# Hash attention followed by a max-out FFN: the projection split on POOL, and pair 1's hash in one pass

## The chip, the cores and the metric

The kernel runs on one core of a Trainium2 chip. A core has five engines that work side by side, each through its own queue in order: TensorE (PE, matrix multiplication), VectorE (DVE), ScalarE (ACT), GpSimd (POOL) and SyncE (SP, here only the issuer of DMAs). They wait for each other on semaphores. The metric is device time in microseconds (us), the median of several runs; lower is better.

## The reference

Attention for 4 batches of 8 heads, 768 positions and 64 dimensions, in which a query sees only the keys of its own hash bucket, and then a feed-forward network on all 3072 tokens:

```python
q_bits = (np.einsum('bhsd,dk->bhsk', q, proj) > 0)       # 6 bits, the same for k
mask = q_bucket[:, :, :, None] == k_bucket[:, :, None, :]
scores = np.where(mask, scale * q @ k.T, -1e9)
attn = exp(scores - max) / (sum + 1e-09)
x = (attn @ v) -> [3072, 512]
h = np.maximum(np.maximum(x @ w1, x @ w2), x @ w3)       # 512 -> 768
out = h @ w_out                                          # 768 -> 512
```

The sign of a projection decides a bit, so the projections are formed to nearly fp32 accuracy: q, k and the projection are each taken apart into an fp16 number and an fp16 remainder.

## The kernel before

**Tiling.** Heads are taken in pairs (b, pr): batch b, pair pr of 0 to 3. For each pair q, k and v are loaded by SP (`load`, L250, 384 KB each). `split_h` (L266 on ACT, L268 on DVE) writes the fp16 part, `split_r` (L273, DVE) the remainder beside it, 24 chunks of 128 positions (2 for q and k, 2 heads, 6 chunks). The chunks are transposed to the tile `T`, with dimension and remainder on 128 partitions: on PE (`pe_T` L292, evacuated by `evac_T` on DVE or ACT, L204 or L202) for batch 0 and the first two pairs of batch 1, by a DMA transpose on SP (`xbar`, L282) for the rest.

**The hash.** `hash_mm` multiplies each chunk of `T` with `PAB`, the 12 columns of the split projection (6 of the fp16 part, 6 of the remainder), which `make_p` (L234 to L239) builds once on DVE. It has two forms. "Summed" (L310) runs two matmuls of 6 columns into the same 6 outputs, 48 per pair; `hash_bits0` then compares them with zero in one DVE instruction. The other (L312) runs one matmul of 12 columns, 24 per pair; `hash_bits` negates the second six (L330) and compares the first six with them (L332). Pairs 0 and 1 of batch 0 are summed, all others take one pass. The bits, scaled, become six more rows of the score product, so that the scores of other buckets vanish in the exponential. For pair (0,0) they go into `S16` and are transposed a second time; for all others they are transposed on PE (L339), written by SP to DRAM (`bit_out`, dr<-bt, L349) and read back into `T` (`bit_in`, T<-dr, L352). This is called the bounce here.

**Attention.** A unit is one score product (L395, two matmuls), one exponential on ACT (`expo`, L401, 128x768) and one product with v (`attend`, L413, six matmuls). There are 192 units, 48 per batch. PSUM holds two score tiles, so the score of unit n waits for the exponential of unit n - 2. `norm_t` and `norm_x` divide by the sums on DVE. The value sums (`vsum` on POOL L363 to L366, `mean_mm` on PE, svp) belong to the masked positions.

**FFN.** `l1` (L478) and `l2` (L496) work on half batches; `l1_evac` takes the maximum on DVE. The weights come in half by half: w1, w2 and w3 as (half, matrix). Most are loaded by a DMA on the POOL queue that converts to fp16 (`load_w`, L541); those named in `plain`, and w_out in three parts, are loaded by SP into the staging tile ws (`stage_w`, L663, two buffers) and converted by POOL (`cast_w`, L204).

**The order.** Nothing is written in order by hand. Every step is a task for `Plan.run`, with a cost in us for its engine, a priority, its inputs and the buffers that it takes and gives. The planner plays the tasks through with these costs and emits on each engine the ready task of the lowest priority number. The result is a fixed program for each queue. A changed cost can therefore change the order of everything behind it. While PE has no ready task before the first score, `keep_warm` emits a filler matmul (wps, L771).

Of the kernel before, what the change touches and what calls it, by code (L numbers as in the profile page):

```python
# [10 lines left out]
AluOp = mybir.AluOpType  # L11
# [16 lines left out]
class Plan:  # L28
# [105 lines left out]
def kernel(  # L134
# [12 lines left out]
    nc = tc.nc  # L147
    B, H, S, D = q.shape
    NBITS = proj.shape[1]
# [9 lines left out]
    NA = 4 * NCH  # L159
# [27 lines left out]
    op = ctx.enter_context(tc.tile_pool(name="op", bufs=OSB))  # L187
# [9 lines left out]
    add = plan.add  # L197
# [8 lines left out]
    p32 = konst.tile([D, NBITS], FP32, name="p32")  # L206
# [16 lines left out]
    PAB = konst.tile([P, 2 * NBITS], FP16, name="PAB")  # L223
# [7 lines left out]
    def make_p(e):  # L231
        ph = konst.tile([D, NBITS], FP16, name="ph")
        pr32 = konst.tile([D, NBITS], FP32, name="pr32")
        nc.vector.tensor_copy(ph[:], p32[:])  # L234
        nc.vector.tensor_tensor(out=pr32[:], in0=p32[:], in1=ph[:], op=AluOp.subtract)
        for o in (0, D):
            for i, src in enumerate((ph, pr32)):
                nc.vector.tensor_scalar(out=PAB[o : o + D, NBITS * i : NBITS * (i + 1)], in0=src[:],
                                        scalar1=1024.0, scalar2=None, op0=AluOp.mult)  # L239


    raws, S16, T, bits, bts, drs, pss = {}, {}, {}, {}, {}, {}, {}
    src = {"q": q, "k": k, "v": v}

    def load(n, b, pr, heads, e):
        h0, h1 = heads
        if (n, b, pr) not in raws:
            raws[n, b, pr] = raw.tile([P, 2, NCH * D], FP32, tag=n + "32", name=n + "32")
        x = src[n][b, 2 * pr + h0 : 2 * pr + h1]
        ENG[e].dma_start(raws[n, b, pr][:, h0:h1, :], x.rearrange("h (p c) d -> p h (c d)", c=NCH))  # L250
# [8 lines left out]
    def split_h(n, b, pr, heads, e):  # L259
        if (b, pr) not in S16:  # L260
            S16[b, pr] = spl.tile([P, NA, 2 * D], FP16, tag="s", name="s")
        a0, a1 = chunks(n, heads)
        o = S16[b, pr][:, a0:a1, 0:D]
        x32 = raw_view(n, b, pr, heads)
        if e == "ACT":
            nc.scalar.activation(o, x32, ActFn.Copy, scale=QS)  # L266
        else:
            ENG[e].tensor_scalar(out=o, in0=x32, scalar1=QS, scalar2=None, op0=AluOp.mult)  # L268
# [12 lines left out]
    def xbar(b, pr, e):  # L281
        nc.sync.dma_start_transpose(operand(b, pr)[:], S16[b, pr][:].rearrange("p a d -> p (a d)"))  # L282

    def bank(key, name):
        pss[key] = mm_ps.tile([P, 512], FP32, tag="mm", name=name)
        return pss[key]
# [10 lines left out]
        copy(e, operand(b, pr)[:, a0:a1, :].rearrange("p a t -> p (a t)"), p16[:, 0 : NCH * P])  # L297

    def hash_mm(b, pr, heads, e):
        hps = bank(("h", b, pr), "hps")  # L300
        summed = 4 * b + pr < 2
        K = NBITS if summed else 2 * NBITS
        for n in range(2):
            for hh in range(*heads):
                for c in range(NCH):
                    a = n * NA2 + hh * NCH + c
                    o = hps[:, a * K : (a + 1) * K]
                    if summed:
                        for i in range(2):
                            nc.tensor.matmul(o, T[b, pr][:, a, :], PAB[:, i * K : (i + 1) * K], start=i == 0, stop=i == 1)  # L310
                    else:
                        nc.tensor.matmul(o, T[b, pr][:, a, :], PAB[:], start=True, stop=True)  # L312

    def hash_bits0(pr, heads, e):
        hv = pss.pop(("h", 0, pr))[:, 0 : NA * NBITS].rearrange("p (n a k) -> p n a k", n=2, k=NBITS)
        sl = slice(heads[0] * NCH, heads[1] * NCH)
        bit = small.tile([P, 2, NA2, NBITS], FP16, tag="bit", name="bit")
        if pr:
            bits[0, pr] = bit
            nc.vector.tensor_scalar(out=bit[:], in0=hv, scalar1=0.0, scalar2=None, op0=AluOp.is_gt)  # L320
            return
        nc.vector.tensor_scalar(out=bit[:, :, sl, :], in0=hv[:, :, sl, :], scalar1=0.0, scalar2=0.5,  # L322
                                op0=AluOp.is_gt, op1=AluOp.subtract)
        nc.vector.tensor_scalar(out=S16[0, pr][:].rearrange("p (n a) d -> p n a d", n=2)[:, :, sl, D : D + NBITS],
                                in0=bit[:, :, sl, :], scalar1=2 * BIT, scalar2=None, op0=AluOp.mult)

    def hash_bits(b, pr, e):
        hv = pss.pop(("h", b, pr))[:, 0 : NA * 2 * NBITS].rearrange("p (a k) -> p a k", k=2 * NBITS)
        neg = small.tile([P, NA, NBITS], FP32, tag="neg", name="neg")
        nc.vector.tensor_scalar(out=neg[:], in0=hv[:, :, NBITS : 2 * NBITS], scalar1=-1.0, scalar2=None, op0=AluOp.mult)  # L330
        bits[b, pr] = bit = small.tile([P, 2, NA2, NBITS], FP16, tag="bit", name="bit")
        nc.vector.tensor_tensor(out=bit[:].rearrange("p n a k -> p (n a) k"), in0=hv[:, :, 0:NBITS], in1=neg[:],  # L332
                                op=AluOp.is_gt)

    def bit_T(b, pr, e):
        bit = bits.pop((b, pr))
        p16 = bank(("b", b, pr), "bps")[:].bitcast(FP16)
        for n in range(2):
            nc.tensor.transpose(p16[0:R, n * P : (n + 1) * P], bit[:, n, :, :].rearrange("p a k -> p (a k)"), iden[:])  # L339
# [183 lines left out]
    def both(dve, act):  # L523
        return [("DVE", dve), ("ACT", act)]
# [7 lines left out]
    for i, (n, pr, heads) in enumerate(order):  # L532
        half = heads != (0, 2)
        loads[n, 0, pr, heads] = add(("SP", 0.45), -400 + i, [], lambda e, n=n, pr=pr, heads=heads: load(n, 0, pr, heads, e),
                                     take=(n,) if heads[0] == 0 else (), xfer=0.55 if half else 1.1)
    mp = add(("DVE", 0.5), -300, [add(("ACT", 0.1), -500, [], lambda e: None, lat=3.2)], make_p)

    def load_w(i, half, e):
        w_ap = (moe_w1, moe_w2, moe_w3)[i].rearrange("(c p) f -> p c f", p=P)
# [21 lines left out]
    def prep(b, pr):  # L561
        U = first_unit[b, pr]
        p0 = U - PRE
        by_pe = b == 0 or b == 1 and pr < 2
        if b > 0:
            for n in "qkv":
                g = divmod(4 * b + pr - GATE, 4)
                if b == 1:
                    g = {("q", 0): (0, 2), ("k", 0): (0, 2)}.get((n, pr), (0, 3) if pr < 3 else (1, 0))
                loads[n, b, pr, (0, 2)] = add(("SP", 0.5), U - 44 + 0.1 * "qkv".index(n), [],  # L570
                                              lambda e, n=n: load(n, b, pr, (0, 2), e), take=(n,), xfer=1.1, pad=2 if 4 * b + pr > 5 else 0.0,
# [31 lines left out]
        ev, both_rs = [], []  # L603
        last = None
        for i, n in enumerate("qk"):
            h = add(both(0.53, 0.72), p0 + 0.1 * i, [loads[n, b, pr, (0, 2)]],
                    lambda e, n=n: split_h(n, b, pr, (0, 2), e), take=("s",) if n == "q" else (),
                    after=[last])
            rs = [add(("DVE", 0.54), p0 + 1 + 0.1 * i, [h, last], lambda e, n=n, hh=hh: split_r(n, b, pr, (hh, hh + 1), e),
                      give=(n,) if hh else ()) for hh in range(2)]  # L610
            last = rs[1]
            if by_pe:
                for hh in range(2):
# [3 lines left out]
                                  give=("mm",)))  # L617
            both_rs += rs
        if not by_pe:
            ev = [add(("SP", 0.6), p0 + 2, both_rs, lambda e: xbar(b, pr, e), pad=4, xfer=4.6, hold=3.4, take=("T",))]  # L620
            xbars[4 * b + pr] = ev[0]
        plan.join(ev, ("s",))
        hm = add(("PE", 1.3 if 4 * b + pr < 2 else 0.67), p0 + 4, ev + [mp], lambda e: hash_mm(b, pr, (0, 2), e), take=("mm",))
        hb = add(("DVE", 0.3 if 4 * b + pr < 2 else 0.62), p0 + 5, [hm],
                 (lambda e: hash_bits(b, pr, e)) if 4 * b + pr >= 2 else (lambda e: hash_bits0(pr, (0, 2), e)), take=("bit",), give=("mm",))
        bT = add(("PE", 0.11), p0 + 6, [hb], lambda e: bit_T(b, pr, e), take=("mm",), give=("bit",))
        be = add(("DVE", 0.28), p0 + 6, [bT], lambda e: bit_evac(b, pr, e), take=("bt",), give=("mm",))
        bo = add(("SP", 0.65), p0 + 7, [be], lambda e: bit_out(b, pr, e), take=("dr",), give=("bt",), xfer=0.05,
# [17 lines left out]
        t = small.tile([P, 1], FP16, tag="hold", name="hold")  # L646
        nc.gpsimd.tensor_copy(t[D : D + NBITS, :], T[b, pr][D : D + NBITS, NA - 1, P - 1 : P])

    plain = ((1, 2),)
    wst_tiles = {}  # L650

    def w_view(w, i):
# [69 lines left out]
    for blk, (b, pr, items) in enumerate(blocks):  # L722
# [6 lines left out]
        for slot in range(2):  # L729
            for j in range(NU):  # L730
                hf, hh = items[slot]
                s = add(("PE", 0.33), u, ready_T[b, pr, hh], lambda e, u=u: score(u, e), take=("sc",), after=[prev_s],
                        give=("T",) if blk == last_block[b, pr] and slot == 1 and j == NU - 1 else ())
# [4 lines left out]
                              take=("av",) if slot == 0 and j == 0 else (), give=("at",))  # L738
                u += 1
        if blk == last_block[b, pr]:  # L740
# [6 lines left out]
                 take=() if b == 0 or (b, hf) in has_xn else ("xn",), after=has_xn.get((b, hf), []) if b else [])  # L747
# [58 lines left out]
```

The softmax here doesn't subtract the row's maximum and nothing guards it: scores larger than these inputs give would overflow.

## Time and profile before

| What | Value |
|---|---|
| Median of 4 runs | 268.09 us (267.53 to 268.93) |
| The profiled execution | 268.34 us, span of its instructions 266.5 us |
| PE, ACT, DVE, POOL busy | 258.1, 196.3, 177.6, 41.1 us |
| Mean granted TensorE clock | 0.993 |
| Bytes moved by DMA | 41.69 MB |
| First score matmul | 13.60 us after the start of the span |

The times of the trace count from the start of the span. A busy share is an average over very different stages: up to 13.6 us the first pair is prepared, until about 48 us there is attention alone, then attention and FFN run interleaved, and from about 212 us there is FFN alone. PE counts as busy while it runs fillers too.

### The profile page before, as it was taken

To read this page: it belongs to the slowest core of one execution; us is meant where nothing else is said; L and a number is where in the kernel's file an instruction comes from. 1 tells how busy PE (TensorE), PEld (TensorE's weight loads), DVE (VectorE), ACT (ScalarE), POOL (GpSimd) and SP (SyncE) were. 2 spreads that over 40 slices of the span, in tenths; PEclk is the share of its full clock that TensorE was granted. 3 is DMA by queue.
4 is the path that set the end of the run, shared out by engine and by line. 5 is a ranking of instruction groups with operands and counts; after the bars stand their busy time and mean duration, and the time that the engine had idled before them with its cause. 6 is when DMAs were issued, how large, how long until landed. Compare 5 with 4: busy or idle time off the path is not lost.

```text
span 266.5 us, 7323 instructions
## 1 busy us (share of the span) xinstructions
PE 258.1 (97%) x2992; PEld 176.5 (66%) x2992; DVE 177.6 (67%) x394; ACT 196.3 (74%) x283; POOL 41.1 (15%) x57
## 2 busy tenths in 40 slices
PE   8799999999989999999999999999999999999995
PEld 8788777767646666677666767765666656555552
DVE  4799789998856898559886796551655535345260
ACT  4689999987926989999989889898899642332422
POOL 1430053173310333003321030000000000000000
PEclk9799999999999999999999999999999999999999
DMA  6994489699998698997995796212130050120303
GB/s 194 369 269 73 137 270 265 183 258 296 222 241 268 199 241 195 208 254 204 181 245 143 232 182 121 54 29 79 42 61 0 4 163 15 42 79 0 121 0 119
DMA packets 67408, 41.69 MB, mean 156 GB/s; under 512 B 48046, under 2 KB 63662, under 8 KB 67374
## 3 DMA queue, kind: packets, MB, share of 16 engines
q1 hardware_dynamic: 64654, 39.26, 57.5%
q0 software_dynamic: 2640, 1.97, 4.8%
q8 instruction: 23, 0.38, 0.6%
q14 instruction: 11, 0.09, 0.1%
q10 hardware_dynamic: 80, 0.00, 0.0%
HBM read 25.72 MB, written 6.84 MB: 122 GB/s over the span
## 4 chain that ended last, share of the span: by engine, by line
PE 78%; DMA 11%; DVE 3%; ACT 2%; POOL 2%; SPq 2%; issue 1%; ACTq 0%; POOLq 0%
PE ps L478 31%; PE sc L395 19%; PE po L496 11%; PE av L413 10%; DMA v<-in_v_dram 3%; PE tps L292 3%; PE hps L312 2%; DMA dr<-bt 2%; DMA q<-in_q_dram 2%; DMA ws<-in_moe_w_dram 2%; DMA ws<-in_moe_w_out_dram 2%; ACT AT L401 2%; SPq L250 1%; DVE s L273 1%; DVE s L268 1%
## 5 line engine op out<-in xcount | busy, mean ns | idle before, releaser
L401 ACT ACTIVATE AT<-sc 128x768 f16<-128x768 f32 x192 | 146.2, 814 | 15.2 <-PE sc L395 13.3
L478 PE MATMUL ps<-xT,w_sb 128*128 128x384 f16 x576 | 106.3, 326 | 0.0
L395 PE MATMUL sc<-T 128*128 128x384 f16 x384 | 93.0, 326 | 0.9 <-ACT AT L401 0.4
L487 DVE TENSOR_TENSOR ht<-ht,ps 128x384 f16<-128x384 f16 x96 | 52.9, 551 | 46.3 <-PE ps L478 43.8
L413 PEld LDWEIGHTS <-AT 128*128 128x128 f16 x1152 | 59.5, 97 | 22.7 <-ACT AT L401 0.2
L478 PEld LDWEIGHTS <-w_sb 128*128 128x128 f16 x576 | 52.7, 98 | 30.8 <-issue 0.7
L413 PE MATMUL av<-vone,AT 128*128 128x65 f16 x1152 | 65.5, 193 | 0.0
L395 PEld LDWEIGHTS <-T 128*128 128x128 f16 x384 | 30.3, 97 | 11.7 <-issue 1.3
L496 PE MATMUL po<-wout_sb,ht 128*128 128x512 f16 (+1 forms) x150 | 33.8, 370 | 1.0 <-POOL wout_sb L204 1.0
L202 ACT CAST ht<-ps 128x384 f16<-128x384 f32 x28 | 13.4, 480 | 26.4 <-DVE ht L487 19.1
L202 ACT COPY osb<-po 128x512 f32<-128x512 f32 (+1 forms) x24 | 13.6, 568 | 19.3 <-PE po L496 19.2
L496 PEld LDWEIGHTS <-ht 128*128 128x128 f16 x150 | 14.1, 98 | 14.8 <-DVE rr L436 1.2
L273 DVE SCALAR_TENSOR_TENSOR s<-q,s 128x384 f16<-128x384 f32 x32 | 21.2, 676 | 4.1 <-ACT s L266 3.9
L363 POOL TENSOR_TENSOR vt<-v 128x384 f32<-128x384 f32 x12 | 13.3, 1111 | 67.2 <-DMA v<-in_v_dram 67.1
L430 DVE TENSOR_TENSOR t<-av,mv 128x390 f32<-128x390 f32 x32 | 17.9, 560 | 7.3 <-PE av L413 7.0
L449 DVE TENSOR_TENSOR xn<-t,rr 128x384 f16<-128x384 f32 x32 | 19.7, 617 | 1.1
L273 DVE SCALAR_TENSOR_TENSOR s<-k,s 128x384 f16<-128x384 f32 x32 | 18.5, 597 | 0.2
L204 DVE CAST ht<-ps 128x384 f16<-128x384 f32 x20 | 11.1, 555 | 10.4 <-PE ps L478 10.1
L292 PE MATMUL tps<-iden,s 128*128 128x128 f16 x168 | 14.7, 233 | 1.7 <-DVE bit L322 1.5
L292 PEld LDWEIGHTS <-s 128*128 128x128 f16 x168 | 11.6, 105 | 2.9 <-DVE s L273 1.7
L202 ACT CAST vone<-v 128x768 f16<-128x768 f32 x12 | 10.0, 834 | 0.9 <-DMA v<-in_v_dram 0.9
L312 PEld LDWEIGHTS <-T 128*128 128x128 f16 x336 | 10.0, 96 | 1.0
(54 smaller groups left out, 144.9 us busy)
## 6 DMA issues: line engine op xcount, KB each, us to landing
v<-in_v_dram SPq DMA_DIRECT2D x16, 384.0 KB
out_dram<-osb SPq DMA_DIRECT2D x23, 256.0 KB
q<-in_q_dram SPq DMA_DIRECT2D x15, 384.0 KB
k<-in_k_dram SPq DMA_DIRECT2D x15, 384.0 KB
w_sb<-in_moe_w_dram POOLq DMA_DIRECT2D x5, 384.0 KB, 10.0
ws<-in_moe_w_out_dram SPq DMA_DIRECT2D x3, 512.0 KB
ws<-in_moe_w_dram SPq DMA_DIRECT2D x2, 384.0 KB
dr<-bt SPq DMA_DIRECT2D x15, 36.0 KB
```

Source lines behind the costliest of these rows:

```text
L202: nc.scalar.copy(o, i)
L273: nc.vector.scalar_tensor_tensor(out=s[:, a0:a1, D : 2 * D], in0=raw_view(n, b, pr, heads), scalar=QS, in1=s[:, a0:a1, 0:D], op0=AluOp.mul ...
L292: nc.tensor.transpose(p16[:, c * P : (c + 1) * P], S16[b, pr][:, a0 + c, :], iden[:])
L312: nc.tensor.matmul(o, T[b, pr][:, a, :], PAB[:], start=True, stop=True)
L395: nc.tensor.matmul(sc[:, i, 0:HQ], t[:, NA2 + hh * NCH + 2 * j + i, :], t[:, hh * NCH + hf * CH : hh * NCH + (hf + 1) * CH, :], start=True ...
L401: nc.scalar.activation(AT[:], scs.pop(u)[:, :, 0:HQ], ActFn.Exp, bias=EXP_BIAS, scale=EXP_SCALE)
L413: nc.tensor.matmul(av[:, o : o + D + 1], AT[:, i, c * P : (c + 1) * P], vones[b % 2][:, 2 * pr + hh, 2 * j + i, 0 : D + 1], start=slot == ...
L430: nc.vector.tensor_tensor(out=t[:, :, :, 0 : D + 1], in0=av[:, :, :, 0 : D + 1], in1=mv, op=AluOp.add)
L449: nc.vector.tensor_tensor(out=xv, in0=t[:, :, :, 0:D], in1=rr[:].to_broadcast([P, 2, CH, D]), op=AluOp.mult)
L478: nc.tensor.matmul(ps[:, 0:HQ], w_sb[i][:, jc, fb * P : (fb + 1) * P], xTs[b, hf][:, jc, :], start=jc == 0, stop=jc == NJ - 1)
L487: nc.vector.tensor_tensor(out=ht[:], in0=ht[:], in1=ps[:, 0:HQ], op=AluOp.max)
L496: nc.tensor.matmul(ps[:, m0:m1], hts[b, hf, fb][:, c * P : (c + 1) * P], wout_sb[:, fb, m0:m1], start=fb == 0, stop=fb == NF - 1)
```

## The change

Four edits in one. `make_p` moves to POOL, and its task is booked there with 1.5 us instead of 0.5 us on DVE. Pair 1 of batch 0 takes the one-pass hash, so that only pair 0 is still summed; its compare is then `hash_bits` with two DVE instructions. The PSUM tiles of the hash are told apart by head, so that both heads of pair 0 can be under way at a time. And `plain` gains (1, 1): the second half of w2 is loaded by SP through the staging tile and converted on POOL, as the second half of w3 was already.

```diff
     def make_p(e):
-        nc.vector.tensor_copy(ph[:], p32[:])
-        nc.vector.tensor_tensor(out=pr32[:], in0=p32[:], in1=ph[:], op=AluOp.subtract)
+        nc.gpsimd.tensor_copy(ph[:], p32[:])
+        nc.gpsimd.tensor_tensor(out=pr32[:], in0=p32[:], in1=ph[:], op=AluOp.subtract)
         for o in (0, D):
             for i, src in enumerate((ph, pr32)):
-                nc.vector.tensor_scalar(out=PAB[...], in0=src[:],
+                nc.gpsimd.tensor_scalar(out=PAB[...], in0=src[:],
                                         scalar1=1024.0, scalar2=None, op0=AluOp.mult)
...
     def hash_mm(b, pr, heads, e):
-        hps = bank(("h", b, pr), "hps")
-        summed = 4 * b + pr < 2
+        hps = bank(("h", b, pr, heads[0]), "hps")
+        summed = 4 * b + pr < 1
...
-    mp = add(("DVE", 0.5), -300, [...], make_p)
+    mp = add(("POOL", 1.5), -300, [...], make_p)
...
-        hm = add(("PE", 1.3 if 4 * b + pr < 2 else 0.67), ...
-        hb = add(("DVE", 0.3 if 4 * b + pr < 2 else 0.62), p0 + 5, [hm],
-                 hash_bits if 4 * b + pr >= 2 else hash_bits0 ...
+        hm = add(("PE", 1.3 if 4 * b + pr < 1 else 0.67), ...
+        hb = add(("DVE", 0.3 if 4 * b + pr < 1 else 0.62), p0 + 5, [hm],
+                 hash_bits if 4 * b + pr >= 1 else hash_bits0 ...
...
-    plain = ((1, 2),)
+    plain = ((1, 1), (1, 2))
```

More of the change, by code (lines that the diff above doesn't have):

```diff
@@ L233, in make_p @@
         pr32 = konst.tile([D, NBITS], FP32, name="pr32")
-        nc.vector.tensor_copy(ph[:], p32[:])
-        nc.vector.tensor_tensor(out=pr32[:], in0=p32[:], in1=ph[:], op=AluOp.subtract)
+        nc.gpsimd.tensor_copy(ph[:], p32[:])
+        nc.gpsimd.tensor_tensor(out=pr32[:], in0=p32[:], in1=ph[:], op=AluOp.subtract)
         for o in (0, D):
             for i, src in enumerate((ph, pr32)):
-                nc.vector.tensor_scalar(out=PAB[o : o + D, NBITS * i : NBITS * (i + 1)], in0=src[:],
+                nc.gpsimd.tensor_scalar(out=PAB[o : o + D, NBITS * i : NBITS * (i + 1)], in0=src[:],
                                         scalar1=1024.0, scalar2=None, op0=AluOp.mult)
@@ L314, in hash_bits0 @@
     def hash_bits0(pr, heads, e):
-        hv = pss.pop(("h", 0, pr))[:, 0 : NA * NBITS].rearrange("p (n a k) -> p n a k", n=2, k=NBITS)
+        hv = pss.pop(("h", 0, pr, heads[0]))[:, 0 : NA * NBITS].rearrange("p (n a k) -> p n a k", n=2, k=NBITS)
         sl = slice(heads[0] * NCH, heads[1] * NCH)
@@ L327, in hash_bits @@
     def hash_bits(b, pr, e):
-        hv = pss.pop(("h", b, pr))[:, 0 : NA * 2 * NBITS].rearrange("p (a k) -> p a k", k=2 * NBITS)
+        hv = pss.pop(("h", b, pr, 0))[:, 0 : NA * 2 * NBITS].rearrange("p (a k) -> p a k", k=2 * NBITS)
         neg = small.tile([P, NA, NBITS], FP32, tag="neg", name="neg")
@@ L535 @@
                                      take=(n,) if heads[0] == 0 else (), xfer=0.55 if half else 1.1)
-    mp = add(("DVE", 0.5), -300, [add(("ACT", 0.1), -500, [], lambda e: None, lat=3.2)], make_p)
+    mp = add(("POOL", 1.5), -300, [add(("ACT", 0.1), -500, [], lambda e: None, lat=3.2)], make_p)
     def load_w(i, half, e):
@@ L622, in prep @@
         plan.join(ev, ("s",))
-        hm = add(("PE", 1.3 if 4 * b + pr < 2 else 0.67), p0 + 4, ev + [mp], lambda e: hash_mm(b, pr, (0, 2), e), take=("mm",))
-        hb = add(("DVE", 0.3 if 4 * b + pr < 2 else 0.62), p0 + 5, [hm],
-                 (lambda e: hash_bits(b, pr, e)) if 4 * b + pr >= 2 else (lambda e: hash_bits0(pr, (0, 2), e)), take=("bit",), give=("mm",))
+        hm = add(("PE", 1.3 if 4 * b + pr < 1 else 0.67), p0 + 4, ev + [mp], lambda e: hash_mm(b, pr, (0, 2), e), take=("mm",))
+        hb = add(("DVE", 0.3 if 4 * b + pr < 1 else 0.62), p0 + 5, [hm],
+                 (lambda e: hash_bits(b, pr, e)) if 4 * b + pr >= 1 else (lambda e: hash_bits0(pr, (0, 2), e)), take=("bit",), give=("mm",))
         bT = add(("PE", 0.11), p0 + 6, [hb], lambda e: bit_T(b, pr, e), take=("mm",), give=("bit",))
```

## The prediction

> **What bounds the kernel now.** I read the page's first two parts, then busy time by stage, then what the TensorE queue (PE) waited for, then the chain that ended last, then the SP queue in order of time. Busy time by stage (PE, weight loads, DVE, ACT, POOL, then granted clock, DMA share, GB/s):
>
> ```profile
> 6.90:10.30 3.40, 1.90 (x47) 1.82 (x45) 1.87 (x6) 2.00 (x4) 0.00 (x0) 1.00 1.04 364
> 10.30:13.70 3.40, 3.40 (x53) 3.40 (x51) 3.34 (x7) 1.97 (x3) 3.17 (x5) 0.50 1.07 377
> 13.70:28.00 14.30, 14.24 (x273) 12.26 (x272) 13.52 (x31) 13.16 (x19) 2.79 (x3) 1.00 0.75 152
> 28.00:48.00 20.00, 19.02 (x321) 14.61 (x317) 17.57 (x43) 19.68 (x28) 6.30 (x9) 1.00 0.85 226
> 48.00:77.00 29.00, 27.53 (x334) 18.55 (x331) 25.83 (x55) 23.14 (x34) 11.50 (x14) 1.00 1.03 247
> 77.00:264.00 187.00, 186.22 (x1934) 120.09 (x1930) 112.19 (x238) 132.90 (x194) 16.61 (x21) 1.00 0.52 126
> ```
>
> PE is busy everywhere, so its work is the first bound, but not the only one. From 28 to 48 ACT is busy 19.68 of 20 us and PE follows its exponentials. From 48 to 77 the DMA engines are full (share 1.03). Only after 77 is it PE alone. The change touches what lies before 77. What PE waited for between 14 and 80 us:
>
> ```profile
> PE po L496 <- POOL wout_sb L204: 1.0, 1, 1.0
> PE svp L376 <- POOL vsum L366: 0.5, 1, 0.5
> PE sc L395 <- ACT AT L401: 0.4, 1, 0.4
> ```
>
> The longest wait is for the last third of w_out. The chain from 40 us says what made that late:
>
> ```profile
> 41.19 6.00 DMA dr<-bt
> ...
> 48.10 5.55 DMA ws<-in_moe_w_dram
> ...
> 61.69 7.87 DMA v<-in_v_dram
> 69.56 0.07 issue
> 69.64 0.75 POOL vt L363
> 70.38 4.62 DMA ws<-in_moe_w_out_dram
> 75.00 0.06 issue
> 75.06 1.05 POOL wout_sb L204
> 76.10 0.04 issue
> 76.14 0.59 PE po L496 x2
> ```
>
> So the end hangs on the SP queue: the bounce of the hash bits of pair (1,0) takes 6.00 us because it is queued behind loads, and everything on SP follows in order until w_out's last third lands at 75.00. PE's later work hangs on the matmul at 76.14. The loads that the bounce waits for, on SP:
>
> ```profile
> 33.00 0.39 SPq L250 DMA_DIRECT2D v<-in_v_dram  x1
> ...
> 35.99 0.47 SPq L250 DMA_DIRECT2D v<-in_v_dram  x1
> 41.19 0.33 SPq L349 DMA_DIRECT2D dr<-bt  x1
> 47.33 0.29 SPq L352 DMA_DIRECT2D T<-dr  x1
> ```
>
> Seven loads are issued from 33.00 to 36.46, then the bounce.
>
> **The change part by part.**
>
> 1. *Projection split to POOL.* DVE loses six instructions of 0.16 us, 4.38 to 5.18 us, one after another about 0.83 us. POOL stands idle from 1.31 to 10.53, so no POOL work is moved past. POOL's nearest rows are the 6x1 copy at 0.18 and the 128x128 adds at 0.46 to 0.66; six at 0.18 to 0.66 take 1.1 to 4.0 us. The Trainium skill (GPSIMD Engine Reference, Performance versus the Vector engine) speaks against this move: elementwise work is roughly twice as slow there, which gives an estimate of 6 x 0.32 = 1.9 us. By the row the split is ready between 5.5 and 8.4 us at the latest, by the page about 6.3; the hash needs it at about 8.2 (next paragraph). I take 0, bounds 0 and +0.2: the hash's bits wait for pair 1's q anyway, and if that cover were gone the cost would be what POOL overruns 8.2 by.
>
> 2. *The front is re-ordered.* The planner books DVE's saved time, and the built program shows the result. Both kernels let DVE pass the residual of pair 1's q (which waits for a load until 8.40 and the ACT split, so 9.27) before the bits of head 0 at 9.75, and PE idles until 10.03. After that point the old order on PE is transposes, two second-pass transposes, fillers, the hash of head 1 and the value sum: 0.57 + 0.64 + 0.64 + 0.43 + 0.62 + 0.67 = 3.57, first score 13.60. The new one has pair 1's transposes 0.57, the hash of head 1 0.62, four groups of second-pass transposes 3 x 0.64 + 0.55, three fillers 0.33 and the value sum at 0.35 (full clock): 4.34, first score about 14.3. Links on ACT and DVE (evacuations of 0.55 to 0.7) fit inside; I take 14.2, +0.6 us. These durations are at half clock. The row shows 0.50 from 10.30 to 13.70, after a stretch with PE busy 1.90 of 3.40. The Trainium skill (TensorE: Matmul & The Clock Gate, The HAM clock gate) says that one idle window of about 3.4 us drops the clock to half, and that the windows run free of the kernel. The new front keeps PE busy about 2.1 of the same 3.4 us (six fillers instead of two there), so by the row it drops again; were the window to count as busy, the work above halves to about 3.1 us and the first score comes at 13.0. I take the row, 14.2.
>
> 3. *Less PE work behind the first score.* Counting both programs: 126 transposes become 114 (two groups of six moved ahead of the first score, 2 x 0.34 = 0.68), and pair 1's hash goes from 48 matmuls (1.18 us at 18.49) to 24 (0.58 at 23.70 for another pair). That is 1.28 us less, 0.60 of it truly removed. Bits of pair 1 cost DVE one operand more: 0.29 becomes 0.30 + 0.31, +0.32 us, beside PE's work (DVE 13.52 of 14.30 busy there, but it has lost more than that to the front). So the gain on PE alone is 1.28 - 0.6 = 0.7 us.
>
> 4. *ACT up to the 13th exponential.* Before: first exponential 14.19, 12 of them at 0.745 and six copies, 13th at 27.79. After: five copies of 0.69 and one split of 0.75 in their place; 14.8 + 12 x 0.745 + 3.45 + 0.75 = 27.9, with the 0.65 us of ACT idle used up. So the late start is recovered by 28 us and nothing more: bits of pair 3 at about 30.3 and the loads from 33.0 as before. Behind it two copies and a cast move later, so ACT is 1 to 1.5 us ahead at the 36th exponential, and without the last-third wait PE would reach that matmul at about 73.8.
>
> 5. *w2's second half through SP instead of the POOL queue.* The planner list of staged weights gains (1,1). SP issues two more loads of 384 KB, placed ahead of q, k, v of pair (1,2); POOL loses one issue (0.7 us) and gains two casts at 0.82, in idle time before the value sums at 41 us (vsum then about 46, needed at 50). POOL's later casts of w3 fall behind the value sum of (1,2), so the 0.48 wait of svp goes; what is late next is w_out, so that is worth 0. The DMA work is the same: from the trace's packets a load is 256 of 1536 B at 77 ns, 1.23 us of 16 engines; a half weight by the POOL queue 512 of 768 B at 78 ns, 2.51 us. But the bounce is on SP's queue and now stands behind nine loads, not seven. At 41.0 us the trace had sent 1375 such packets; nine loads leave 2304 - 1375 = 929. While the remaining POOL load shares (about 118 packets per us for SP, 4 us) 472 go, the other 457 at 245 per us take 1.9: clear at 46.9, the bounce's packets 0.3, landing 0.7 after (0.9 before): 47.9, against 47.19. So +0.7 us. Bounds: -0.5 if loads land sooner with less POOL traffic, +2 if the queue clears only when the whole 13.6 us of DMA work from 34 on is done (47.6) and the write is slow. Behind it the order on SP is unchanged (two w3 loads, q, k, v, bits, transpose, two w_out, q, k, v, transpose, w_out's last third), with the DMA engines full, so the shift is carried to 75.7 for the landing.
>
> The sum: the matmul that was at 76.14 is at about 76.8, and PE's work behind it is the same in both (186.4 us by count). PE's earlier 2.3 us are swallowed there. Profiled execution 268.34 (span 266.5 and 1.8 around it) + 0.7 = 269.0; the median of the runs lies 0.25 lower, so 268.8.
>
> **The rivals.**
>
> *PE's shorter list counts.* If the front keeps full clock, first score, bits of pair 3 and loads all come 1.0 to 1.2 us sooner, w_out lands at 74.5 instead of 75.7, and the time is 268.8 - 1.2 = 267.6; with a bounce that isn't delayed either, 266.9, and with w_out out of the way altogether 268.1 - 2.3 = 265.8. For it: 1.28 us less PE work, wait of svp gone. Against: the half-clock row, and that nothing makes the SP chain shorter.
>
> *Slower: the bounce behind nine loads.* Place: the write of the bits on SP at 41.2 us. It decides from the point where the read-back is issued after 48.7 instead of 47.33: then w_out's third lands beyond 76.4 and the end is more than 1.34 later. Price at the upper bound +2.0: 270.1, with a second bounce delayed alike (the pair (1,1), written at 51.25) 271. For it: the 6.00 us that seven loads already cost, DMA at 0.85 to 1.03. Against: the same bytes in total.
>
> *The one-pass hash does nothing for the time.* Then 1.18 to 0.58 is hidden by ACT's 19.68 of 20 and the time differs only by the DMA order; this is contained in the first case.
>
> **How the numbers follow.** A difference of 0.5%, 1.34 us, is about what a measurement of this kernel can tell from no change. The likely case (0.5; its own range 267.5 to 270.0) gives mostly "same", with 0.1 beyond on the slow side. PE's list (0.25): 0.2 faster, 0.05 same. The bounce (0.25): slower. Faster 0.2, same 0.45, slower 0.35. Range 266.4 to 271.0: both rivals without their ends.
>
> **What would show it.** In the changed profile: first score near 14.2 and half clock ahead of it; the 13th exponential near 27.9; pair 1's hash as 24 matmuls in 0.58; POOL's split done before 8.2; the bounce of (1,0) landing at 47.9 rather than 47.2; PE's wait for wout_sb grown from 1.0 to 2 or 3 us and the matmul behind it at 76.8. The prediction is wrong if that wait is gone or shrinks (PE's list counts), or if the read-back is issued after 48.7.

## The result, and the profile after

| | before | changed |
|---|---|---|
| median of the runs on one chip, us | 268.33 (265.09 to 271.67) | 269.12 (267.17 to 272.37) |
| ratio, 95% interval | | 1.0049 (1.0031 to 1.0068) |
| profiled execution: time, span, granted clock | 268.34, 266.5, 0.993 | 268.59, 266.8, 0.998 |

Ratios and their intervals are taken over the fast runs alone and medians over all runs, so the two can differ. The change makes the kernel about 1.3 us slower, by the ratio; the forecast was 268.8 us, +0.7 in its sum. The number came out, and by luck: most of the steps to it did not, and what was measured in their place happened to add up to about the same.

The granted clock is needed to read the two profiles side by side: the execution profiled of before contains one 3.4-us window at half clock, and the one profiled of the changed kernel contains none. Busy time by stage of the changed kernel, in the order PE, weight loads, DVE, ACT, POOL, then clock, DMA share, GB/s:

```profile
6.90:10.30 3.40, 2.92 (x78) 2.76 (x76) 3.37 (x9) 2.93 (x4) 0.00 (x0) 1.00 1.02 343
10.30:13.70 3.40, 2.97 (x43) 2.41 (x41) 3.37 (x9) 3.00 (x4) 3.31 (x5) 1.00 1.07 375
```

The second row had 0.50 in the clock column before; it has 1.00 now. In the first row PE is busy for 2.92 of 3.40 us, where it was 1.90 before and the prediction took 2.1. POOL builds the projection early enough (POOL's timeline; first and last of six):

```profile
3.48 0.18 POOL L234 CAST ph<-p 64x6 f16<-64x6 f32 x1 [2.17 <-DMA p<-in_proj_dram]
...
5.32 0.23 POOL L238 TENSOR_SCALAR PAB<-pr 64x6 f16<-64x6 f32 x1
```

What PE waited for in the first 80 us (total, times, longest):

```profile
PE sc L395 <- DMA T<-dr: 0.7, 1, 0.7
PE po L496 <- POOL wout_sb L204: 0.5, 1, 0.5
PE tps L292 <- ACT T L202: 0.5, 1, 0.5
```

The wait for w_out is halved, the one for the value sum of 0.5 is gone, and there is a new one: a score of pair 1 waits for the first bounce, `T<-dr`. SP's queue shows that bounce (18.74 to 23.94), the third (30.37 to 32.09) and the one of pair (1,0), with the first and last of the nine loads that this last one stands behind:

```profile
18.74 0.38 SPq L349 DMA_DIRECT2D dr<-bt  x1
23.94 0.28 SPq L352 DMA_DIRECT2D T<-dr  x1
...
30.37 0.32 SPq L349 DMA_DIRECT2D dr<-bt  x1
32.09 0.29 SPq L352 DMA_DIRECT2D T<-dr  x1
32.43 0.39 SPq L250 DMA_DIRECT2D v<-in_v_dram  x1
...
37.63 0.44 SPq L250 DMA_DIRECT2D v<-in_v_dram  x1
41.24 0.32 SPq L349 DMA_DIRECT2D dr<-bt  x1
46.92 0.29 SPq L352 DMA_DIRECT2D T<-dr  x1
```

Before, the first bounce was this:

```profile
21.59 0.38 SPq L349 DMA_DIRECT2D dr<-bt  x1
23.89 0.28 SPq L352 DMA_DIRECT2D T<-dr  x1
```

The bits of pair 1 are now written 2.85 us sooner and read back at the same time. The chain that ended last, around w_out and its matmul:

```profile
69.26 4.13 DMA ws<-in_moe_w_out_dram
73.45 1.05 POOL wout_sb L204
74.54 0.59 PE po L496 x2
```

That matmul was at 76.14, so the changed kernel is 1.60 us ahead there, and yet its span is 0.25 longer. From the trace, three stretches: up to that matmul, from there to the start of the last matmul, and from there to the end of the span (called the tail below):

| us | up to w_out's matmul | behind it | tail | span |
|---|---|---|---|---|
| before, profile on record | 76.14 | 187.02 | 3.37 | 266.54 |
| changed | 74.54 | 187.92 | 4.33 | 266.79 |
| before again (`x0_before`, no half clock) | 74.61 | 186.87 | 3.40 | 264.88 |

Against the profile on record: -1.60 + 0.90 + 0.96 = +0.25 (rounded parts). Against the same kernel at full clock: -0.08 + 1.05 + 0.93 = +1.90. The loss lies in places where the prediction had put nothing. What PE waited for behind 78 us in the changed kernel:

```profile
PE ps L478 <- DVE ht L487: 0.4, 1, 0.4
PE sc L395 <- ACT AT L401: 0.2, 1, 0.2
```

### The profile page after: what moved, and what is told of

Its sections match the earlier page's. It is cut to its first block, busy times and chain, and to the rows that moved or that the text cites. A ratio compares the mean times of both kernels' runs of the same rounds, so it can differ in the third digit from the quotient of the medians.

```text
span 266.8 us, 7269 instructions
## 1 busy us (share of the span) xinstructions
PE 257.2 (96%) x2962; PEld 174.1 (65%) x2962; DVE 177.4 (66%) x386; ACT 197.6 (74%) x286; POOL 44.8 (17%) x64
## 4 chain that ended last, share of the span: by engine, by line
PE 70%; DMA 13%; DVE 6%; ACT 3%; POOL 3%; issue 2%; SPq 2%; ACTq 0%; POOLq 0%
PE ps L478 29%; PE sc L395 17%; PE po L496 11%; PE av L413 9%; DMA ws<-in_moe_w_dram 3%; DMA v<-in_v_dram 3%; DMA q<-in_q_dram 3%; DVE s L273 2%; ACT AT L401 2%; PE hps L312 2%; DMA T<-dr 2%; DMA k<-in_k_dram 2%; DMA ws<-in_moe_w_out_dram 2%; POOL vt L363 1%; SPq L250 1%
## 5 line engine op out<-in xcount | busy, mean ns | idle before, releaser
L395 PEld LDWEIGHTS <-T 128*128 128x128 f16 x384 | 30.4, 97 | 12.2 <-issue 1.4
L202 ACT CAST ht<-ps 128x384 f16<-128x384 f32 x33 | 15.8, 479 | 28.0 <-DVE ht L487 20.6
L202 ACT COPY osb<-po 128x512 f32<-128x512 f32 (+1 forms) x22 | 12.5, 567 | 19.3 <-PE po L496 19.3
L273 DVE SCALAR_TENSOR_TENSOR s<-q,s 128x384 f16<-128x384 f32 x32 | 22.0, 705 | 4.3 <-ACT s L266 4.2
L273 DVE SCALAR_TENSOR_TENSOR s<-k,s 128x384 f16<-128x384 f32 x32 | 19.5, 628 | 0.5 <-ACT s L266 0.5
L292 PE MATMUL tps<-iden,s 128*128 128x128 f16 x168 | 14.2, 226 | 1.2 <-ACT T L202 0.5
L204 DVE CAST ht<-ps 128x384 f16<-128x384 f32 x15 | 8.3, 555 | 9.1 <-PE ps L478 8.9
L292 PEld LDWEIGHTS <-s 128*128 128x128 f16 x168 | 10.9, 101 | 3.0 <-DVE s L273 1.7
L312 PEld LDWEIGHTS <-T 128*128 128x128 f16 x360 | 10.7, 96 | 1.0
L312 PE MATMUL hps<-PAB,T 128*128 128x12 f16 x360 | 11.2, 168 | 0.0
```

The costliest lines, as they stand in the source:

```text
L202: nc.scalar.copy(o, i)
L273: nc.vector.scalar_tensor_tensor(out=s[:, a0:a1, D : 2 * D], in0=raw_view(n, b, pr, heads), scalar=QS, in1=s[:, a0:a1, 0:D], op0=AluOp.mul ...
L292: nc.tensor.transpose(p16[:, c * P : (c + 1) * P], S16[b, pr][:, a0 + c, :], iden[:])
L395: nc.tensor.matmul(sc[:, i, 0:HQ], t[:, NA2 + hh * NCH + 2 * j + i, :], t[:, hh * NCH + hf * CH : hh * NCH + (hf + 1) * CH, :], start=True ...
```

## The experiments

**The kernel before at full clock.** The same file once more.

> The kernel before once more, for a profile in which the front keeps full clock (the profile on record had 0.50 from 10.30 to 13.70). If that half-clock window is what set its front, the first exponential starts about 12.5 to 13.0 instead of 14.19, yet the read-back of the first bounce stays at about 23.9 (it was 23.89 and 23.94 in the two kernels) and the 13th exponential at about 27.3, so the last matmul is 0.5 to 1.5 us earlier than 263.17 and the span about 265.3. The tail from last matmul start to the last SP event stays 3.3 us. A rival theory, that the first score carries through, gives a 13th exponential near 26.5 and a last matmul near 261.8.

Measured: 266.65 us, span 264.9, clock 1.0; first exponential 12.58, 13th 27.17, last matmul 261.48. The bounce on SP and the end of the chain:

```profile
19.90 0.38 SPq L349 DMA_DIRECT2D dr<-bt  x1
24.18 0.28 SPq L352 DMA_DIRECT2D T<-dr  x1
```

```profile
73.53 1.05 POOL wout_sb L204
...
74.61 0.59 PE po L496 x2
```

The first score is at 12.02, 1.58 us sooner than in the profile on record, and the first read-back is at 24.18, no sooner. As the first theory expected, the bounce does not follow the front, and the 13th exponential is near its 27.3, 0.62 us sooner than in the profile on record. At the end the theory was too cautious: the last matmul is 1.69 us sooner than 263.17, not 0.5 to 1.5, and near the 261.8 of the rival. In front of w_out's matmul the changed kernel leads this execution by 0.08 us only. So nearly all of its lead of 1.60 belongs to the execution of before that was on record. Of 157 executions of before, 47 have a mean granted clock below 0.9955 (one such window in 267 us), with a median of 269.57 us; the 96 at 0.9985 or more have 267.40. The changed kernel's runs of `x4_after` below 0.9955 are 8 of 22, so the change does not remove the window: the execution profiled happened to have none.

**The changed kernel again.** No edit.

> The changed kernel once more, for a second profile. If the 13th score waits for the first bounce as a rule, it starts at 27.0 to 27.3 again though the first score is near 12.6; if the lead at w_out's last third (74.5 against 76.1) is the rule, the last matmul ends 0.5 to 1 us earlier than in before, and the time is made longer by what follows it. If it was chance, one of the two is gone. Ratio 1.003 to 1.007.

Measured: 269.72 us, ratio 1.0047 (1.0016 to 1.0079). Profile: w_out's matmul at 73.96, behind it 188.04, tail 4.24, wait for wout_sb 1.4. The two losses, behind the matmul and in the tail, are there again, and the last matmul, at 262.00, is 1.17 us before the one on record. The front is not the same in two executions: the first score is at 12.51 and 11.62, the 13th at 27.07 and 25.62. The expectation that the 13th score waits for the first bounce as a rule failed: PE has no such wait here.

**The tail.** The trace of the changed kernel has 129 DMAs on SP, that of before 127, because w2's second half is two more. (The texts put on record below count two more for every kernel: 131 and 129, and 137 for `z1_tail`, which has 135.) The trace also shows which completion semaphore each DMA has: they take eight in turn, so two more DMAs shift which of the eight the last two stores get, and SP waits for the eight one after another at the end. Two edits test this, one on each kernel:

```diff
 # z1_tail, on the changed kernel: six stores in halves, 135 DMAs; z2_shift, on before: two stores, 129
-        nc.sync.dma_start(rows[:, hf * CH + c, m0:m1], t[:, m0:m1])
+        h = (m0 + m1) // 2          # z1: (b, hf) in ((2, 1), (3, 0)); z2: (b, hf) == (3, 0) and c < 2
+        nc.sync.dma_start(rows[:, hf * CH + c, m0:h], t[:, m0:h])
+        nc.sync.dma_start(rows[:, hf * CH + c, h:m1], t[:, h:m1])
```

> The changed kernel with six output stores sent in two halves each, so that SP starts 137 DMAs instead of 131 and the last two stores carry the same two of the eight completion semaphores as in the kernel before (129 DMAs). The order on PE, VectorE, ScalarE and GpSimd is untouched. Theory of the tail: the changed kernel's end, 4.26 us from its last matmul to its last SP event, goes back to about 3.3, and the ratio to the kernel before falls by 0.9 us / 268 = 0.0034, to about 1.001 to 1.002. Rival (the tail is only where a delay from further ahead shows, or is chance): tail stays at 4.2 and ratio at 1.005.

> The kernel before with two output stores of the last matrix group's first part sent in two halves each: 131 SP DMAs as in the changed kernel, nothing else moved. Theory of the tail: the last stores change their completion semaphores, the tail grows from 3.3 to about 4.2 us, and the ratio is about 1.003 (0.9 us). Rival: two small stores more cost nothing, ratio 1.000, tail 3.3.

Measured: `z1_tail` 268.94 us, ratio 1.0020 (0.9994 to 1.0046), tail 3.36; `z2_shift` 269.64 us, ratio 1.0054 (1.0026 to 1.0081), tail 4.31. The views below give, of four kernels, the span and the last copy by ACT, in the order before on record, changed, `z1_tail`, `z2_shift`:

```profile
core 0 of [0], span 266.5 us
...
263.52 0.37 ACT osb L202
```

```profile
core 0 of [0], span 266.8 us
...
262.81 0.37 ACT osb L202
```

```profile
core 0 of [0], span 268.9 us
...
265.94 0.37 ACT osb L202
```

```profile
core 0 of [0], span 267.0 us
...
263.03 0.37 ACT osb L202
```

From the copy's end to the span's end: 2.6, 3.6, 2.6 and 3.6 us. The copy starts 0.35 us behind the start of the last matmul in all four. In all six profiles with 129 DMAs the tail (from the last matmul's start) is 4.23 to 4.40; in the eight others, with 127 or 135, it is 3.36 to 3.87. SP's own records show how, in us from the start of the last matmul (from the trace):

```
                    last two stores   the waits for the eight end at
before, 127         0.10  0.75        1.13 1.50 1.59 1.65 1.71 1.78 2.06 2.48
x1_pool, 127        0.10  0.88        1.27 1.33 1.39 1.45 1.51 1.71 2.13 2.86
changed, 129        0.42  0.86        3.05 3.11 3.17 3.24 3.30 3.36 3.42
z2_shift, 129       0.10  0.88        2.05 3.04 3.10 3.16 3.23 3.29 3.35 3.41
```

Before, the last store's semaphore is the last of the eight, so the last landing is waited for last. In the changed kernel and in `z2_shift` it is the second of the eight (the first wait of the changed kernel is for two of them), and six waits of 0.06 each still follow it. Of the 0.94 us between the last figures of before and changed, 0.37 is this series, and it comes and goes with the number of DMAs. The other 0.57 is a last landing that is seen later, and that is not due to the number alone: `x1_pool`, `x2_hash` and `p2_leanth`, with 127 DMAs, have it at 2.86, 2.98 and 2.98, and so their tails of 3.76 to 3.87. In all of these, as in the six with 129, the last store is issued at 0.85 to 0.88 and not at 0.75. What delays that store, and why 0.1 us there becomes 0.4 to 0.6 at the landing, is not settled by these runs. In the times, `z1_tail`'s point estimate lies below the changed kernel's by 0.0029, 0.8 us, the size of the tail; the two intervals overlap. `z2_shift` is clearly slower than before, and its interval holds the 0.0034 that its tail would cost. So the profiles show the place, and the times only the direction.

The profile of `z1_tail` itself has its half-clock window elsewhere, after a wait of PE for w_out:

```profile
PE po L496 <- POOL wout_sb L204: 1.8, 1, 1.8
```

```profile
77.80:81.20 3.40, 3.40 (x23) 1.50 (x20) 0.85 (x3) 0.81 (x2) 0.00 (x0) 0.50 0.93 214
```

which makes its span 268.9; its median does not rest on that execution.

**What holds the first bounce.** While the bits of pair 1 wait, the POOL queue's first weight loads fill the DMA engines. Packets started in each microsecond of the changed kernel's profile, from the trace:

```
us from           18   19   20   21   22   23
weights, 768 B   258  249  261  194   43    6
bits, 256 B        0    0    0   76   52   16
loads, 1536 B      4    0    0    0    0    0
```

The bits are written at 18.74 and their first packet goes at 21.31. They do not wait behind SP's own loads: these have sent their last packets by 19. The experiment holds the POOL loads of the first halves of w2 and w3 back until that bounce is read back:

```diff
         # bit_in, behind the read-back of (b, pr) == (0, 1); the loads are left out at the start
+        if (b, pr) == (0, 1):
+            hold(0, 1, e)
+            for x in deferred:
+                load_w(*x, None)
```

> The changed kernel with the POOL queue's loads of the first halves of w2 and w3 held back until the first bounce of hash bits has been read back; all else in its order. Theory that these weight packets hold the first bounce back: its read-back is issued at about 20.5 instead of 23.94, PE's wait of 0.7 us for the transposed operand goes, the 13th exponential comes about 1 us earlier than 27.67, at 26.7. What that is worth at the end depends on the later loads: if PE's work counts, ratio about 1.001; if the weights' later arrival is paid back in the loads from 32 us on, 1.005 as without it or worse. Rival: the bounce is held by something else and stays at 23.9.

Measured: 272.12 us, ratio 1.0096 (1.0058 to 1.0133), the slow end of what was expected. On SP:

```profile
18.60 0.38 SPq L349 DMA_DIRECT2D dr<-bt  x1
21.27 0.28 SPq L352 DMA_DIRECT2D T<-dr  x1
...
29.38 0.32 SPq L349 DMA_DIRECT2D dr<-bt  x1
34.77 0.29 SPq L352 DMA_DIRECT2D T<-dr  x1
35.10 0.99 SPq L250 DMA_DIRECT2D v<-in_v_dram  x1
```

The read-back is at 21.27 for 23.94 (20.5 was expected), and the 13th exponential at 26.68, as expected: the weight packets held the bounce. But the weights have to come some time. They now collide with the third bounce, which takes 5.39 us (29.38 to 34.77) where it took 1.72 (30.37 to 32.09); the loads that started at 32.43 start at 35.10, and w_out's matmul is at 77.77. A gain of 1 us at 27 became a loss of 3.2 at 75. In the ratio the loss against the changed kernel is 0.0047, 1.3 us, and the two intervals just overlap.

**The parts of the change by themselves.** `x1_pool`: before with only the projection split on POOL. `x2_hash`: before with only pair 1's hash in one pass. `x3_plain`: before with only w2's second half through SP. `y1_noplain`: the changed kernel without that. The first three also name the hash's PSUM tiles by head; in `x3_plain`, PE, DVE and ACT run the same instructions in the same order as before, so this moves nothing there. Each is one line or two of the diff of the change:

```diff
-    mp = add(("DVE", 0.5), -300, ...        # x1_pool, and nc.vector -> nc.gpsimd in make_p
+    mp = add(("POOL", 1.5), -300, ...
-        summed = 4 * b + pr < 2              # x2_hash, and its costs in the plan
+        summed = 4 * b + pr < 1
-    plain = ((1, 2),)                        # x3_plain; the reverse in y1_noplain
+    plain = ((1, 1), (1, 2))
```

> The kernel before with the projection split on POOL alone (booked at 1.5 there), pair 1 still summed. The front is re-ordered much as in the changed kernel. Theory SP: an earlier first score gives nothing, as the first bounce waits for the first three weight loads until about 23.9; ratio 1.000 to 1.003. Theory PE: 0.68 us of transposes move ahead of the first score, ratio 0.996 to 0.999.

> The kernel before with only the hash of pair 1 in one pass (24 matmuls for 48, one compare operand more on VectorE); projection split on VectorE and w2's second half on the POOL queue as before, 129 SP DMAs. Theory (the end hangs on landings ahead of w_out's matmul, so PE's 0.6 us is swallowed, and the tail is that of before, 3.3 us): ratio 0.999 to 1.001. Rival (PE's list counts): 0.6 us / 268 off, ratio 0.998. Rival (every part costs something, by a re-ordered plan): 1.003.

> The kernel before with the staged second half of w2 alone; the order on PE, DVE and ACT is that of before. Theory SP (the end hangs on the SP chain, the bounce of (1,0) stands behind nine loads): read-back of (1,0) 0.2 to 0.7 us later than the 47.33 of before, w_out's last third and PE's matmul behind it as much later, ratio 1.001 to 1.003. Theory PE (only PE's list counts): no difference, ratio 1.000. Theory rest (the two loads cost elsewhere, later on the queues): ratio above 1.004 with the matmul behind w_out not later.

> The changed kernel with the second half of w2 back on the POOL queue; PE, DVE and ACT in the order of the changed kernel. Theory SP: the bounce is earlier by what the two loads cost it, ratio 1.002 to 1.004 against before (the changed kernel has 1.005). Theory PE: as the changed kernel, 1.005. Theory rest: all of the slowdown is from the staged half, ratio 1.000 or below.

| | ratio, 95% interval | w_out's matmul | behind it | tail |
|---|---|---|---|---|
| `x1_pool` | 1.0031 (1.0004 to 1.0059) | 74.99 | 188.42 | 3.76 |
| `x2_hash` | 1.0203 (1.0143 to 1.0264) | 77.63 | 191.98 | 3.84 |
| `x3_plain` | 1.0065 (1.0037 to 1.0094) | 75.23 | 187.31 | 4.23 |
| `y1_noplain` | 1.0038 (1.0005 to 1.0072) | 75.15 | 189.82 | 3.37 |

No part gains, and the parts do not add: the sum of the three alone would be 1.030, the whole change is 1.0049. `x2_hash`, which takes 0.6 us of work from PE, is 5.4 us slower, which none of its theories had. The reason is in the order: with the changed booked times the planner puts SP's transpose ahead of the write of the bits of pair (1,1). SP in `x2_hash`, then in `x0_before`:

```profile
51.20 7.20 SPq L282 DMA_TRANSPOSE T<-s  x1
58.47 0.53 SPq L349 DMA_DIRECT2D dr<-bt  x1
```

```profile
50.78 0.39 SPq L349 DMA_DIRECT2D dr<-bt  x1
53.18 4.22 SPq L282 DMA_TRANSPOSE T<-s  x1
```

Those bits go out 7.7 us later, w_out's matmul is 3.0 us later, and behind it PE has waits of its own, the longest of them this (PE's waits from 78 us on):

```profile
PE sc L395 <- ACT AT L401: 2.7, 1, 2.7
```

That the swap is the cause of the whole 5.4 us was read from the traces and not tried by itself; the profile also has a half-clock window at 91.8 us. In the whole change the front differs again and the bits are ahead of the transpose (49.85 and 53.57).

In `x3_plain` the bounce of pair (1,0) does what step 5 of the prediction expected:

```profile
40.66 0.32 SPq L349 DMA_DIRECT2D dr<-bt  x1
48.31 0.29 SPq L352 DMA_DIRECT2D T<-dr  x1
```

7.65 us against 6.14 in the profile on record of before and 5.32 in `x0_before`. Its span is 1.89 us longer than that of `x0_before`: 0.62 up to w_out's matmul, 0.44 behind it, 0.83 in the tail. That is more than its first theory allowed (read-back 0.2 to 0.7 us later, ratio up to 1.003). In `y1_noplain`, with seven loads ahead of the bounce and not nine, the bounce is no faster than in the changed kernel:

```profile
41.16 0.32 SPq L349 DMA_DIRECT2D dr<-bt  x1
46.95 0.29 SPq L352 DMA_DIRECT2D T<-dr  x1
```

So its ratio lies where the first theory had put it, but not for that theory's reason. With 127 DMAs it has the tail of before, and it loses behind w_out's matmul instead. `x1_pool` came out at the upper end of its first theory; its second, 0.996 to 0.999, is outside the interval.

**Does PE's work count ahead of w_out's matmul?** `p1_lean` takes 3.3 us of hash from PE. `p2_leanth` also takes the load of w_out's last third away, and `w1_after` takes that load alone from the changed kernel:

```diff
 # p1_lean and p2_leanth, hash_mm: 2 wide matmuls for 48 or 24
+        if 1 <= 4 * b + pr <= 6:
+            for n in range(2):
+                rhs = T[b, pr][:, n * NA2 : n * NA2 + 2, :].rearrange("p a t -> p (a t)")
+                nc.tensor.matmul(hps[:, n * NA2 * K : (n + 1) * NA2 * K], T[b, pr][:, n * NA2 + NA2 - 1, :],
+                                 rhs[:, 0 : NA2 * K], start=True, stop=True)
+            return
 # p2_leanth and w1_after, stage_w
+        if (w, i) == ("o", 2):
+            wst_tiles[w, i] = o_prev[0]     # the tile of the second third
+            return
```

> The kernel before with the hash of pairs 1 to 6 (three of batch 0, three of batch 1) done by two wide matmuls each, so the hash bits are not the reference's; all the rest in its order, same DMAs. PE loses about 3.3 us of work (1.18 + 5 x 0.60 - 6 x 0.15) ahead of the matmul behind w_out's last third, five times what the change takes away. Theory (landings set that matmul's time): the matmul stays within 0.5 us of 74.6 (full clock), PE's idle time ahead of it grows by about 3 us, ratio 0.998 to 1.001. Rival (PE's list counts): the matmul comes 3 us sooner, ratio 0.988.

> The kernel with the lean hash and, besides, without the load of w_out's last third: its cast reads the second third's tile again, so that third of w_out is wrong; one store is halved so that the number of SP DMAs stays 129. If it is w_out's landing that swallows PE's saving, the matmul comes up to 3 us sooner and the ratio falls to about 0.988 to 0.992; if the saving is swallowed further ahead (at the bounces of hash bits, or q, k, v of later pairs), it stays like the lean hash alone, 0.998 to 1.001.

> The changed kernel without the load of w_out's last third (the cast reads the second third's tile again, so that third of w_out is wrong), one store halved so that SP still starts 131 DMAs; order on all engines as in the changed kernel. PE's wait for wout_sb (0.5 us in the first profile of the changed kernel, 1.4 in the second) goes. Theory: the matmul behind the last third comes 0.5 to 1.4 us sooner and the ratio falls from 1.0049 by that, to 1.000 to 1.003; tail stays at 4.2. Rival (that wait only covers another): ratio stays at 1.004 to 1.005.

Measured: `p1_lean` 1.0018 (0.9983 to 1.0053), `p2_leanth` 0.9999 (0.9968 to 1.0030), `w1_after` 1.0045 (1.0017 to 1.0072). Five times the PE work that the change saves brings nothing: 0.988, or 3 us, is far outside the interval. In the profile of `p1_lean` w_out's matmul is at 74.86. PE's idle time from its first instruction to 74 us is 5.44 us for 3.56 in `x0_before`, 1.9 more and not the 3 that were expected, and the rest of the saving went into a half-clock window, 28.5 to 31.9, behind a longer wait for the first bounce:

```profile
PE sc L401 <- DMA T<-dr: 1.7, 1, 1.7
```

```profile
28.40:31.90 3.50, 3.50 (x30) 2.47 (x30) 1.63 (x6) 2.53 (x4) 0.00 (x0) 0.52 0.73 228
```

Without w_out's last third it gets no better, so w_out's landing is not the only sink: the saving is gone before; the bounces and loads are where the waits of `p1_lean` lie. `w1_after` says the same of the changed kernel. The wait for wout_sb is gone from its profile, whose matmul is at 73.18, but the time is that of the changed kernel (1.0045 for 1.0049). The rival that this wait only covers another held. Its one profile, with a span of 264.9, is shorter than its runs.

## Why the prediction was right, and where its steps were not

*Step 1, the split on POOL: right.* Six instructions end at 5.55, and no engine waits for them. The move itself is not free: by itself, with the new order that it brings, it is at 1.0031. From the first start to the last end they take 2.07 us; the estimate by the Trainium skill (GPSIMD Engine Reference, Performance versus the Vector engine) was 1.9, the bounds by row 1.1 to 4.0.

*Step 2, first score at 14.2 by a half-clock front: wrong in its base.* It took the 0.50 in the row as a property of the front, but it belongs to some executions only. The first score came at 12.51. Against the profile of before without the window, 12.02, it is 0.49 us later: the re-ordering was sized about rightly (+0.6). The alternative named there, 13.0, was the better choice, and its sum was off: the items at half clock in 4.34 make 3.99, so at full clock they and the value sum take about 2.3 us and not 3.1, which from 10.03 gives 12.4. The Trainium skill (TensorE: Matmul & The Clock Gate, The HAM clock gate) says that the windows run free of the kernel, and the traces here agree. Within a profile the changes of the clock lie whole multiples of 3.41 us apart, and the first change to full clock falls at 6.90 and 5.58 us in two executions of before, at 6.21 and 5.55 in two of the changed kernel. Half-clock windows of 3.41 us start at 10.3, 28.5, 40.2, 77.8 and 91.8 us in five of the profiles; the others have none between the first change to full clock and the last matmul. The skill's idle window, from which the prediction argued, is not what the traces show: in the 3.41 us ahead of these five, PE was busy for 0.97 to 1.91 us, and windows of 1.7 to 2.0 us in other profiles were not followed by half clock.

*Step 3, 1.28 us less on PE: right as a count, and right that nothing of it arrives.* Pair 1's hash is 24 matmuls in 0.58:

```profile
20.63 0.58 PE hps L312 x24
```

The two instructions of its compare take 0.303 and 0.307 us, as said. `p1_lean` shows that, in the kernel before, even 3.3 us would not arrive. The rival "PE's shorter list counts" falls with it.

*Step 4, the 13th exponential at 27.9: 27.67, for another reason.* The prediction summed ACT's work from a late start. In the profile on record the 13th score waits 0.7 us for the read-back of the first bounce, which is at 23.9 in both kernels and at 22.8 to 24.8 in all runs but `z3_late`. `z3_late` brought the read-back to 21.27 and the exponential to 26.68. In `x4_after` PE does not wait for it, and the exponential comes at 26.21, so the near hit is in part chance. The loads came 0.57 us sooner than in the profile on record, 32.43 for 33.00 (32.11 in `x0_before`), and not as before.

*Step 5, +0.7 us on the bounce of (1,0), carried to w_out: mis-sized for the whole change.* From the first of the loads to the read-back it took 14.49 us for 14.33, so +0.16, and 14.68 in `y1_noplain` without the two loads; in `x3_plain`, alone, the mechanism showed with +1.5 on the bounce. Read-back at 46.92 and the matmul at 74.54, for 47.9 and 76.8. The slower rival's point of decision, a read-back after 48.7, was reached by `z3_late` alone of the kernels with the whole change (51.10): there w_out's matmul is at 77.77 and the time 272.12, slower as that rival said, but because of the held weights.

*The prediction's own sign of being wrong.* It was to be wrong if the wait for wout_sb shrank. On record it went from 1.0 to 0.5 us, in `x4_after` to 1.4, in `x0_before` it is 0.3; the 2 to 3 us of the forecast were reached nowhere. By this test the path through w_out failed as the reason. That does not make the rival right: w_out's matmul is where `x0_before` has it.

*What the sum left out.* "PE's work behind it is the same in both" holds by count (1947 matmuls) and not by time: 187.92 and 188.04 for 187.02 and 186.87. PE's idle time there is 0.78 us for 0.22, with the two waits shown above, 0.4 for `ht` of DVE and 0.2 for an exponential. The other 0.3 to 0.5 is spread over the matmuls. Single profiles scatter here: `z2_shift`, with the order of before, has 186.90, and `w1_after`, with the changed order, 187.43. And the tail, for which the prediction had no term, grew by 0.96. These two replace step 5 as the loss. So +0.7 was predicted from step 5 alone, and +0.25 between the profiles came from -1.60, +0.90 and +0.96. With the half-clock window taken out it is +1.9 between profiles, and by the ratio +1.3. That the forecast lies between these is luck.

*What stays open.* How much of the loss behind w_out's matmul is due to which evacuation was not separated, and nothing was tried to take it away. The later last landing in the tail has no shown cause either. `z1_tail` leaves 0.2%, within its interval of nothing.

## What to carry to other kernels

Look at the granted clock of the profiled execution beside those of the other runs before taking its stages as the usual ones: here executions with a half-clock window took 2.2 us more in the median than those at full clock, more than the change. The idle time of PE that goes ahead of such a window is part of that. A transfer that two queues share moves the end only if the other queue's bytes move too, and they have to go somewhere: the first bounce was 2.7 us faster, w_out's matmul 3.2 us later, and the kernel no faster. Where a planner orders the work, an edit is the new order it causes; compare the programs' queues first, and count the DMAs, since the last store's place among the completion semaphores was worth 0.37 us of a tail that grew by 0.9.

## What the runs showed of the hardware that was not expected

A small write on SP's queue, 144 packets of 256 B, issued at 18.74 while 768-B weight packets of the POOL queue ran at about 260 a microsecond, sent no packet for two microseconds and was read back 5.2 us after its issue; with the weights held back, 2.7. A half-clock window came not only at the start: in `p1_lean` it stands behind a wait of PE of 1.7 us, in `z1_tail` behind one of 1.8. PE was not idle for the window ahead of it, but busy for 1.6 of 3.41 us in both. And two DMAs more in the middle of a kernel lengthened its last stage, from 3.4 to 4.3 us in the profiles, without any change of the instructions in that stage; 0.37 us of it is SP's waits behind the last landing.
